# Polysketch attention with a sentence-level expert layer: k and q of the first batch in two loads each, kv turned whole, and output stores of two quarters each

## The chip, the cores and the metric

The kernel runs on one core of a Trainium2 chip. The metric is the device time of one execution in microseconds (us), lower is better. The profile's span of the same execution is 2.0 to 2.1 us shorter than the time.

Each run is marked fast or slow; slow is a run over 1.5% above the fastest of the same kernel. Ratios below are the mean time of one kernel's fast runs over the mean of the fast runs of the kernel before from the same rounds, so they are not quite the ratios of the medians quoted beside them.

## The reference, cut to what matters

```python
def phi(x):                                   # [B, H, S, 32] -> [B, H, S, 64], r = 8
    a = einsum('rd,bhsd->bhsr', S1, x)
    b = einsum('rd,bhsd->bhsr', S2, x)
    return einsum('bhsi,bhsj->bhsij', a, b).reshape(..., r * r)
q_p, k_p = phi(q), phi(k)
kv  = einsum('bhsf,bhsd->bhfd', k_p, v)
z   = k_p.sum(axis=2)
x   = (q_p @ kv) / (q_p @ z + 1e-6)           # per head; then [B, S, H*32]
e   = argmax(x.mean(axis=1) @ w_gate)         # one expert for a whole sentence
out = gate * (relu(x @ w1[e]) @ w2[e])        # [4, 1088, 128] float32
```

There are four batches, four heads and 1088 tokens. The output is 2.23 MB. The experts' weights cannot be loaded before a batch's attention is finished, since the gate picks them.

## The kernel before: the parts that matter

The kernel is a list of operations in a fixed order with a fixed engine for each. It lays a batch's 1088 tokens out as 32 groups (`pp`) of 34 (`x`); the 34 are cut into four quarters of 9, 9, 8 and 8. A chunk of 128 tokens is four quarters by 32 groups, so in the output tile `ob` a quarter lies on 32 partitions.

```python
X0  = (0, 9, 18, 26)                 # where a quarter starts among the 34
LEN = (9, 9, 8, 8)
...
o_s = [plan.add({"ACTQ": 0.4}, lambda: load_s(nc.scalar, 0), bus=0.1),     # S1 from the ACT queue
       plan.add({"POOL": 1.0}, lambda: load_s(nc.gpsimd, 1))]              # S2 from the POOL queue
...
def x_out(eng, i):                                  # attention's result as bf16: tokens in the order (chunk, quarter, group)
    n = LEN[2 * i]
    x = T(xbf)[:].rearrange("p (c a t) -> p a c t", a=4, t=32)[:, 2 * i:2 * i + 2, 0:n]
...
def store(queue, quarters, s=s, ob=ob):             # s: one of three thirds of a batch's chunks
    dst = out[b].rearrange("(pp x) d -> pp (x d)", pp=32)
    for a in quarters:
        m = min(3, LEN[a] - 3 * s)
        lo = X0[a] + 3 * s
        queue.dma_start(dst[:, 128 * lo:128 * (lo + m)], T(ob)[32 * a:32 * a + 32, 0:128 * m])
```

There are 48 stores, four for each third of a batch, each of 32 rows of 1536 bytes (1024 in some). There are four `ob` buffers.

Some words of this document, which counts batches from 0: the *sketch* is the product of k or q with the matrices S1 and S2, which are turned (transposed) on PE first; a *turn* of k or q is a transpose on DVE. The *key products* and *query products* are the outer products `a_i * b_j` of `phi`, made on POOL and DVE. The *numerators* are the products `q_p @ kv` on PE. The engines are PE (TensorE, matrix products), DVE (VectorE), ACT (ScalarE) and POOL (GpSimd). SP, ACT and POOL also issue DMA transfers, each on a queue of its own, and the transfers run on the core's 16 DMA engines.

Of the kernel before, what the change touches and what calls it, by code (L numbers as in the profile page):

```python
# [77 lines left out]
def kernel(  # L78
# [12 lines left out]
    nc = tc.nc  # L91
# [25 lines left out]
        kvr=([P, 64], FP32), kvs=([P, 2, H, 32], FP32), zs=([P, 32], FP32), wq=([P, 96], FP32),  # L117
# [48 lines left out]
    def pre_turned():  # L166
        for i in range(kinds["kT"]):
# [6 lines left out]
    o_pre_turned = plan.add({"DVE": 0.5}, pre_turned)  # L174
    plan.add({"ACT": 1.5}, lambda: nc.scalar.activation(out=tiny[:, 0:4], in_=tiny[:, 4:8], func=AF.Exp),
             after=[o_pre_dve])
    o_s = [plan.add({"ACTQ": 0.4}, lambda: load_s(nc.scalar, 0), bus=0.1),
           plan.add({"POOL": 1.0}, lambda: load_s(nc.gpsimd, 1))]
# [10 lines left out]
    WARM = 5  # L189
    plan.add({"PE": 1.17}, warm_up, after=[o_pre_dve], uses=[wslot], n=2 * WARM)  # L190
# [30 lines left out]
    def attention(b):  # L221
# [4 lines left out]
        def turned(src, ld, tr):  # L226


            def load(lo, hi):
                nc.sync.dma_start(T(ld)[:, 32 * lo:32 * hi],  # L230
                                  src[b].rearrange("h (pp x) d -> (h pp) (x d)", pp=32)[:, 32 * lo:32 * hi])

            whole = b or src is q
            parts = [(0, 34)] if whole else [(0, 18), (18, 34)]
            loads = [add({"SP": 0.4}, lambda lo=lo, hi=hi: load(lo, hi), bus=1.75 if whole else 0.065 * (hi - lo),
                         uses=[ld]) for lo, hi in parts]

            def turn(a, m, n):
                nc.vector.transpose(  # L239
                    out=T(tr)[:, 0:n, a:a + m, :].rearrange("p c a t -> p a c t"),  # L240
                    in_=T(ld)[:, 32 * X0[a]:32 * (X0[a] + m * n)].rearrange("p (a c d) -> p a c d", a=m, d=32))

            turns = [(0, 2, 9, 0), (2, 2, 8, -1)]
            return [add({"DVE": 0.08 + 0.0388 * m * n}, lambda a=a, m=m, n=n: turn(a, m, n),
                        after=[loads[i], o_pre_turned], uses=[ld, tr]) for a, m, n, i in turns]
# [41 lines left out]
        def sketch(ps, tr, w, moving, lo, hi, halves):  # L287

            for c in range(lo, hi):
                for o in halves:  # L290
                    nc.tensor.matmul(cols(ps, w, c)[o:o + 64],  # L291
                                     T(tr)[:, c, o // 32:o // 32 + 2].rearrange("p a t -> p (a t)"), moving)
# [5 lines left out]
        def sketches(ps, tr, w, moving, ts, each, after, uses):  # L298

            if b >= SPLIT:  # L300
                return [plan.add({"PE": 0.1 + 9 * each}, lambda: sketch(ps, tr, w, moving(), 0, 9, (0, 64)),
                                 after=ts + after, uses=[tr] + ps + uses, n=72, form="128x64")]
            first = plan.add({"PE": 0.05 + 4.5 * each}, lambda: sketch(ps, tr, w, moving(), 0, 9, (0,)),
                             after=[ts[0]] + after, uses=[tr] + ps + uses, n=36, form="128x64")
            return [plan.add({"PE": 0.05 + 0.5 * (hi - lo) * each},
                             lambda lo=lo, hi=hi: sketch(ps, tr, w, moving(), lo, hi, (64,)),
                             after=[ts[1], first], uses=[tr, ps[i]] + uses, n=4 * (hi - lo), form="128x64")
                    for i, (lo, hi) in enumerate(thirds)]
# [6 lines left out]
        ks = sketches(kps, kT, 64, lambda: s12[:].rearrange("p t h r -> p (t h r)"), kt, 1.15 / 9, [o_sk], [])  # L315
# [48 lines left out]
        def k_v(s):  # L364
            run.append(s)
            for i, c in enumerate(range(3 * s, 3 * s + 3)):
# [6 lines left out]
               for s in range(3)]  # L373
        kr = add({"DVE": 0.2, "ACT": 0.25}, lambda eng: copy(eng, T(kvr)[:], T(kvps)[:, 0:64]), after=kvm,
                 uses=[kvps, kvr])

        def turn_kv():

            for u in range(2):
                for a in range(4):  # L380
                    nc.tensor.matmul(T(kvt)[32 * a:32 * a + 32, 128 * u:128 * u + 128],
                                     T(kvr)[:, 32 * u:32 * u + 32], ident[:])

        tk = add({"PE": 0.5}, turn_kv, after=[kr], uses=[kvr, kvt], n=32, form="128x32")
# [7 lines left out]
        qs = sketches(qps, qT, 96, lambda: T(wq)[:], qt, 1.38 / 9, [wo, o_sx], [wq])  # L392
# [102 lines left out]
    def experts(b, st):  # L495
# [21 lines left out]
        for k, (i, lo, hi) in enumerate(pieces):  # L517
# [3 lines left out]
            costs = {"POOL": 0.08 + 1.0 * part, "ACT": 0.2 + 0.85 * part, "DVE": 0.12 + 0.62 * part}  # L521
            cw.append(add(costs, lambda eng, i=i, lo=lo, hi=hi: cast(eng, i, lo, hi), after=[lw], uses=[wf, wbf]))
        for s in range(3):
# [56 lines left out]
            def store(queue, quarters, s=s, ob=ob):  # L580
                dst = out[b].rearrange("(pp x) d -> pp (x d)", pp=32)
                for a in quarters:
                    m = min(3, LEN[a] - 3 * s)
                    lo = X0[a] + 3 * s
                    queue.dma_start(dst[:, 128 * lo:128 * (lo + m)], T(ob)[32 * a:32 * a + 32, 0:128 * m])

            if tail:
                add({"SP": 0.9}, lambda store=store: store(nc.sync, (0, 1)), after=oe, uses=[ob], bus=0.4)
                add({"ACTQ": 0.9}, lambda store=store: store(nc.scalar, (2, 3)), after=oe, uses=[ob], bus=0.4)
            else:  # L590
                add({"SP": 1.8}, lambda store=store: store(nc.sync, range(4)), after=oe, uses=[ob], bus=0.8)

    sts = [attention(b) for b in range(B)]
    for b in range(B):
# [3 lines left out]
        6, 14, 5, 3, 15, 0, 39, 4, 8, 2, 1, 32, 7, 16, 9, 10, 17, 18, 11, 72, 12, 21, 13, 19, 24, 20, 22, 27, 23, 41,  # L598
        28, 40, 29, 26, 30, 31, 116, 42, 25, 35, 45, 43, 50, 34, 73, 46, 33, 51, 44, 74, 85, 36, 48, 37, 47, 54, 52,
        75, 38, 57, 118, 60, 92, 49, 55, 117, 77, 53, 58, 119, 160, 76, 63, 67, 56, 81, 79, 59, 121, 82, 120, 83, 61,  # L600
        125, 124, 87, 62, 93, 123, 64, 94, 84, 126, 162, 136, 80, 95, 66, 161, 65, 78, 180, 68, 96, 98, 88, 69, 127,
        163, 99, 122, 97, 204, 70, 128, 100, 86, 71, 138, 165, 206, 164, 101, 89, 168, 129, 137, 169, 90, 103, 139,
        91, 167, 170, 208, 102, 106, 205, 171, 142, 104, 182, 140, 236, 238, 143, 237, 172, 141, 181, 239, 105, 223,
        144, 224, 183, 107, 207, 166, 146, 145, 242, 108, 184, 240, 186, 243, 131, 185, 148, 187, 132, 241, 130, 188,
        225, 133, 173, 212, 209, 147, 226, 134, 213, 245, 135, 244, 149, 190, 189, 227, 151, 246, 228, 109, 150, 192,
        247, 152, 210, 248, 111, 193, 110, 174, 211, 176, 195, 112, 175, 191, 153, 113, 177, 196, 249, 114, 115, 178,
        194, 155, 251, 229, 154, 179, 214, 230, 156, 215, 216, 231, 217, 157, 197, 294, 158, 250, 292, 159, 219, 198,
        257, 199, 233, 258, 279, 285, 252, 218, 280, 286, 281, 232, 282, 268, 234, 259, 269, 283, 260, 220, 235, 284,
        200, 270, 221, 201, 272, 271, 266, 273, 288, 222, 202, 287, 295, 267, 253, 255, 254, 289, 293, 337, 275, 256,
        290, 335, 276, 203, 326, 311, 327, 309, 312, 291, 261, 310, 315, 262, 316, 322, 313, 323, 263, 314, 296, 264,  # L610
        298, 274, 297, 299, 265, 300, 318, 301, 338, 328, 324, 336, 329, 319, 302, 325, 277, 317, 303, 356, 278, 320,
        343, 357, 331, 344, 354, 332, 355, 321, 345, 352, 346, 330, 353, 369, 333, 306, 371, 370, 358, 334, 304, 372,
        359, 305, 341, 307, 339, 342, 361, 308, 362, 340, 360, 367, 363, 365, 368, 349, 348, 364, 366, 347, 373, 350,
        375, 378, 351, 374, 376, 377, 380, 379,
    )
    ENGINES = (
        "2332153200230144220000122333010240001014220000121212222222323222011502124220113330102400010142201222"
        "2222332220210212422011333020240001014220121222233322201102124220113330202400010242201212222333222011"
        "0212414342010202010001401010101000240101010100014424301010202000140201010200024020101010002442410102"
        "010100014010202010002401010101000144242020202010002402010102000240101010100011145"  # L620
    )
    PLACES = (
        0, 1, 11, 0, 0, 0, 0, 0, 0, 0, 0, 1, 10, 0, 0, 1, 0, 0, 11, 0, 10, 0, 1, 0, 0, 0, 0, 0, 1, 12, 0, 0, 1, 2, 0,
        1, 1, 1, 0, 1, 1, 1, 1, 0, 1, 0, 1, 0, 1, 1, 1, 1, 0, 1, 1, 1, 1, 0, 1, 1, 2, 0, 0, 2, 2, 2, 1, 0, 0, 0, 2,
        10, 0, 12, 0, 0, 0, 0, 1, 0, 0, 0, 0, 0, 0, 2, 0, 0, 0, 2, 0, 3, 3, 3, 1, 1, 1, 1, 1, 0, 1, 1, 1, 0, 1, 1, 1,
        1, 1, 1, 1, 1, 1, 0, 1, 1, 1, 2, 1, 0, 0, 2, 1, 2, 2, 0, 0, 2, 1, 1, 1, 1, 1, 1, 1, 0, 1, 0, 2, 1, 0, 0, 1,
        1, 3, 1, 2, 0, 2, 0, 0, 1, 0, 1, 1, 2, 1, 1, 0, 1, 0, 0, 2, 0, 3, 0, 0, 3, 0, 1, 2, 2, 0, 0, 0, 2, 1, 2, 0,
        0, 2, 2, 1, 1, 0, 0, 1, 3, 1, 1, 0, 0, 2, 1, 0, 0, 2, 1, 1, 2, 0, 1, 1, 1, 2, 2, 1, 2, 0, 1, 3,
    )
    WIDE = (156, 200)  # L630
    FILLS = {
        8: (2, 1), 18: (1, 3), 28: (3, 4), 30: (3, 2), 42: (2, 2), 119: (2, 2), 83: (3, 2), 169: (3, 4), 223: (3, 0),
# [38 lines left out]
```

## Time and profile before

| | before |
|---|---|
| time, first three runs | 83.62, 84.59, 87.48 us |
| the profiled execution (a slow one) | 89.07 us, span 87.0 |
| PE busy, share of the span | 74.5 us, 86% |
| output stores | 48, of 48 KB mostly, issued in 0.42 us each |

The prediction shows the main lines of this profile. Two more are of use later. They are the two DMA rows of the page: the span is cut into 40 slices, and for each the first row gives the mean busy share of the core's 16 DMA engines in tenths, the second what they moved in GB/s.

```profile
DMA  1996707038946869931611248693429723424441
GB/s 24 341 265 141 254 0 244 20 82 202 335 166 222 242 222 261 231 91 40 185 39 36 50 107 279 177 347 124 107 71 275 258 74 78 109 64 104 110 111 36
```

Look at the last eight slices, where only output stores are left: 64 to 111 GB/s, at a share of 0.2 to 0.4 (the very last slice is the end of the work, with less). Sixteen engines are far from full there, and PE is busy in most of these slices: the stores go as fast as the work before them delivers.

### The profile page before, as it was taken

To read this page: it belongs to the slowest core of one execution; us is meant where nothing else is said; L and a number is where in the kernel's file an instruction comes from. 1 tells how busy PE (TensorE), PEld (TensorE's weight loads), DVE (VectorE), ACT (ScalarE), POOL (GpSimd) and SP (SyncE) were. 2 spreads that over 40 slices of the span, in tenths; PEclk is the share of its full clock that TensorE was granted. 3 is DMA by queue.
4 is the path that set the end of the run, shared out by engine and by line. 5 is a ranking of instruction groups with operands and counts; after the bars stand their busy time and mean duration, and the time that the engine had idled before them with its cause. 6 is when DMAs were issued, how large, how long until landed. Compare 5 with 4: busy or idle time off the path is not lost.

```text
span 87.0 us, 3463 instructions
## 1 busy us (share of the span) xinstructions
PE 74.5 (86%) x1460; PEld 53.9 (62%) x1460; DVE 58.7 (67%) x131; ACT 42.7 (49%) x94; POOL 36.4 (42%) x37
## 2 busy tenths in 40 slices
PE   3929999999969997999099999999999979999700
PEld 1207837887539856576075747688787856889600
DVE  2403264299995998999999978478964865585200
ACT  3300100233307424948136567679979977945120
POOL 4202595039999999999739700040000000000000
PEclk9999579999999999999999999999999999999999
DMA  1996707038946869931611248693429723424441
GB/s 24 341 265 141 254 0 244 20 82 202 335 166 222 242 222 261 231 91 40 185 39 36 50 107 279 177 347 124 107 71 275 258 74 78 109 64 104 110 111 36
DMA packets 10990, 13.32 MB, mean 153 GB/s; under 512 B 1504, under 2 KB 9184, under 8 KB 10976
## 3 DMA queue, kind: packets, MB, share of 16 engines
q1 hardware_dynamic: 10688, 13.05, 51.4%
q8 instruction: 11, 0.18, 0.9%
q10 hardware_dynamic: 256, 0.07, 0.3%
q14 instruction: 3, 0.02, 0.1%
q0 software_dynamic: 32, 0.00, 0.0%
HBM read 10.89 MB, written 2.23 MB: 151 GB/s over the span
## 4 chain that ended last, share of the span: by engine, by line
PE 48%; DVE 23%; DMA 12%; issue 7%; ACT 4%; SPq 1%; ACTq 0%
DMA wf<-in_moe_w_dram 12%; PE pt L554 12%; PE ps L533 9%; PE ps L447 7%; DVE wbf L217 5%; DVE phT L438 5%; PE ps L291 5%; PE pt L291 4%; PE ps L639 3%; PE pt L187 2%; DVE bc L404 2%; DVE kT L239 2%; DVE den L410 2%; DVE den L409 2%; ACT xbf L460 2%
## 5 line engine op out<-in xcount | busy, mean ns | idle before, releaser
L543 ACT ACTIVATE hT<-ps 128x768 bf16<-128x768 f32 (+1 forms) x33 | 23.9, 762 | 8.3 <-PE ps L533 8.0
L554 PE MATMUL pt<-wbf,hT 128*128 128x128 bf16 (+1 forms) x288 | 20.5, 220 | 2.9 <-DVE wbf L217 2.4
L554 PEld LDWEIGHTS <-hT 128*128 128x128 bf16 (+1 forms) x288 | 17.9, 99 | 6.8 <-issue 4.4
L533 PE MATMUL ps<-xbf,wbf 128*128 128x384 bf16 (+1 forms) x96 | 19.4, 318 | 1.0 <-ACT wbf L215 0.6
L280 POOL TENSOR_TENSOR phk<-kab 128x768 f32<-128x768 f32 x12 | 17.8, 1509 | 2.2 <-DVE kab L217 2.2
L545 DVE TENSOR_SCALAR hT<-ps 128x768 bf16<-128x768 f32 (+1 forms) x15 | 13.9, 946 | 6.2 <-PE ps L533 5.6
L280 POOL TENSOR_TENSOR phq<-qab 128x768 f32<-128x768 f32 x10 | 14.9, 1511 | 6.6 <-DVE qab L413 6.6
L438 DVE STREAM_TRANSPOSE phT<-phq 128x768 f32<-128x768 f32 x12 | 11.1, 948 | 0.0
L533 PEld LDWEIGHTS <-wbf 128*128 128x128 bf16 x96 | 8.1, 99 | 4.7 <-issue 0.8
L460 ACT ACTIVATE xbf<-ps 128x512 bf16<-128x512 f32 (+1 forms) x7 | 4.3, 616 | 5.9 <-PE ps L447 5.9
L447 PE MATMUL ps<-phT,kvs 32*32 32x256 f32 (+1 forms) x256 | 6.5, 399 | 0.7 <-DVE phT L438 0.7
L291 PE MATMUL ps<-wq,qT 128*64 128x96 f32 x120 | 6.8, 250 | 0.3 <-DVE qT L239 0.2
L217 DVE CAST wbf<-wf 128x1024 bf16<-128x1024 f32 x5 | 5.9, 1185 | 1.4 <-DMA wf<-in_moe_w_dram 1.4
L291 PEld LDWEIGHTS ps<-wq,qT 128*64 128x64 f32 x120 | 5.7, 137 | 1.6 <-ACT hT L543 0.5
L239 DVE STREAM_TRANSPOSE kT<-ld 128x576 f32<-128x576 f32 (+1 forms) x8 | 5.8, 729 | 0.2 <-DMA ld<-in_k_dram 0.2
L239 DVE STREAM_TRANSPOSE qT<-ld 128x512 f32<-128x512 f32 (+1 forms) x8 | 5.6, 717 | 0.0
L639 PE MATMUL ps<-warm 128*128 128x512 bf16 x17 | 5.5, 424 | 0.0
L567 ACT ACTIVATE ob<-pt,gate 64x128 f32<-64x128 f32 (+3 forms) x10 | 4.2, 446 | 2.4 <-issue 1.3
L291 PE MATMUL ps<-s,kT 128*64 128x64 f32 x120 | 5.2, 230 | 0.0
L291 PEld LDWEIGHTS ps<-s,kT 128*64 128x64 f32 x120 | 4.5, 142 | 0.8 <-DVE den L409 0.4
L570 DVE TENSOR_SCALAR ob<-pt,gate 128x384 f32<-128x384 f32 (+2 forms) x7 | 3.7, 554 | 1.7 <-DMA out_dram<-ob 1.2
L447 PEld LDWEIGHTS ps<-phT,kvs 32*32 32x32 f32 x256 | 3.4, 103 | 2.3 <-DVE phT L438 0.8
(87 smaller groups left out, 74.2 us busy)
## 6 DMA issues: line engine op xcount, KB each, us to landing
wf<-in_moe_w_dram SPq DMA_DIRECT2D x7, 512.0 KB, 5.8
ld<-in_q_dram SPq DMA_DIRECT2D x4, 544.0 KB, 5.2
out_dram<-ob SPq DMA_DIRECT2D x40, 48.0 KB, 1.6
ld<-in_k_dram SPq DMA_DIRECT2D x3, 544.0 KB, 3.6
vld<-in_v_dram SPq DMA_DIRECT2D x8, 144.0 KB, 4.0
vld<-in_v_dram SPq DMA_DIRECT2D x8, 128.0 KB, 4.1
wf<-in_moe_w_dram SPq DMA_DIRECT2D x2, 256.0 KB, 4.4
ld<-in_k_dram SPq DMA_DIRECT2D x1, 288.0 KB, 2.7
```

Source lines behind the costliest of these rows:

```text
L217: (nc.vector if eng == "DVE" else nc.gpsimd).tensor_copy(o, i)
L239: nc.vector.transpose(out=T(tr)[:, 0:n, a:a + m, :].rearrange("p c a t -> p a c t"), in_=T(ld)[:, 32 * X0[a]:32 * (X0[a] + m * n)].rearran ...
L280: nc.gpsimd.tensor_tensor(out=T(ph)[:, 3 * s:3 * s + 3, :, :].rearrange("p c h (i j) -> p (c h) i j", i=R), in0=view[:, 0].unsqueeze(3).to ...
L291: nc.tensor.matmul(cols(ps, w, c)[o:o + 64], T(tr)[:, c, o // 32:o // 32 + 2].rearrange("p a t -> p (a t)"), moving)
L438: turns = [add({"DVE": 0.97}, lambda s=s: nc.vector.transpose(out=T(phT)[:, :, 3 * s:3 * s + 3, :].rearrange("p f c t -> p c f t"), in_=T( ...
L447: nc.tensor.matmul(T(nps[a // 2])[32 * h:32 * h + 32, a % 2, 0:32 * LEN[a]], T(kvs)[32 * a:32 * a + 32, u, h, :], T(phT)[32 * a:32 * a + 3 ...
L460: nc.scalar.activation(out=x, in_=y, func=AF.Copy, accum_out=T(pool)[:, i:i + 1])
L533: nc.tensor.matmul(T(hp)[:, t, 0:w], T(wbf)[:, 0, 128 * j:128 * j + 128], T(xbf)[:, 384 * s:384 * s + w])
L543: nc.scalar.activation(out=o, in_=i, func=AF.Relu)
L545: nc.vector.tensor_scalar(out=o, in0=i, scalar1=0.0, scalar2=None, op0=MAXOP)
L554: nc.tensor.matmul(T(ops)[0:n, 128 * i:128 * i + 128], T(hT)[:, j, 128 * i:128 * i + n], T(wbf)[:, 1, 128 * j:128 * j + 128], start=(j == ...
L639: nc.tensor.matmul(singles[bank][:, :] if bank < 2 else pairs[bank - 2][:, 0, :], warm[:, 0:128], warm[:, :])
```

## The change

Its intent, as the diff lets one read it: bring the first sketch and the first query products forward, keep the weight casts of the first two batches off DVE, turn kv in two transposes instead of sixteen small products, and halve the number of stores. The diff, cut to its core:

```diff
-    o_s = [plan.add({"ACTQ": 0.4}, lambda: load_s(nc.scalar, 0), bus=0.1),
-           plan.add({"POOL": 1.0}, lambda: load_s(nc.gpsimd, 1))]
+    o_s = [plan.add({"ACTQ": 0.5}, lambda: load_s(nc.scalar, 0), bus=0.1),
+           plan.add({"ACTQ": 0.5}, lambda: load_s(nc.scalar, 1), bus=0.1)]
...
-            whole = b or src is q
+            whole = b > 0
             parts = [(0, 34)] if whole else [(0, 18), (18, 34)]
... (the first batch's sketches go by thirds of the chunks, over both token halves at once)
-                for a in range(4):
-                    nc.tensor.matmul(T(kvt)[32 * a:32 * a + 32, 128 * u:128 * u + 128],
-                                     T(kvr)[:, 32 * u:32 * u + 32], ident[:])
+                nc.tensor.transpose(T(kvt)[:, 128 * u:128 * u + 128], T(kvr)[:, u].rearrange("p a f -> p (a f)"), ident[:])
...
-            costs = {"POOL": 0.08 + 1.0 * part, "ACT": 0.2 + 0.85 * part, "DVE": 0.12 + 0.62 * part}
+            costs = {"POOL": 0.08 + 1.0 * part, "ACT": 0.2 + 0.85 * part}
+            if b > 1:
+                costs["DVE"] = 0.12 + 0.62 * part
...
-                    m = min(3, LEN[a] - 3 * s)
-                    lo = X0[a] + 3 * s
-                    queue.dma_start(dst[:, 128 * lo:128 * (lo + m)], T(ob)[32 * a:32 * a + 32, 0:128 * m])
+                    n, m, x = LEN[a], min(3, LEN[a] - 3 * s), X0[a]
+                    queue.dma_start(
+                        dst[:, 128 * x:128 * (x + 2 * n)].rearrange("pp (a y) -> a pp y", a=2)[
+                            :, :, 384 * s:384 * s + 128 * m],
+                        T(ob)[32 * a:32 * a + 64, 0:128 * m])
...
-                add({"SP": 1.8}, lambda store=store: store(nc.sync, range(4)), after=oe, uses=[ob], bus=0.8)
+                add({"SP": 0.9}, lambda store=store: store(nc.sync, (0, 2)), after=oe, uses=[ob], bus=0.8)
... (and a new order of operations and assignment of engines)
```

The line `"pp (a y) -> a pp y"` lists the destination as 2 quarters by 32 groups by 384 elements, with the 2 outermost.

## The prediction

> **What bounds the kernel now.** I read the busy table first: no engine is full over the whole span, so the kernel has stages. The slices and the group table then say which engine sets which stage, and the timeline shows the joints.
>
> ```profile
> span 87.0 us, 3463 instructions
> PE 74.5 (86%) x1460; PEld 53.9 (62%) x1460; DVE 58.7 (67%) x131; ACT 42.7 (49%) x94; POOL 36.4 (42%) x37
> PE   3929999999969997999099999999999979999700
> POOL 4202595039999999999739700040000000000000
> PEclk9999579999999999999999999999999999999999
> ```
>
> The columns are fortieths of the span, 2.18 us each. Up to about 19 us the start is a chain of waits. From 19 to 49 us POOL is full (22 products of 1.5 us). From 44 us to the end PE is full with the expert products. The joints, from the timeline (start, duration, engine, line, what; the bracket is the idle time before it and what ended that):
>
> ```profile
> 6.37 0.25 PE L193 MATMUL pt<-ident,sraw 16*32 16x16 f32 x8 [1.71 <-issue]
> 18.88 1.51 POOL L280 TENSOR_TENSOR phq<-qab 128x768 f32<-128x768 f32 x1 [4.64 <-DVE qab L413]
> 20.66 1.27 PE L291 MATMUL ps<-s,kT 128*64 128x64 f32 x36
> ...
> 38.56 4.46 POOL L280 TENSOR_TENSOR phq<-qab 128x768 f32<-128x768 f32 x3
> 40.40 3.17 DVE L217 CAST wbf<-wf 128x1024 bf16<-128x1024 f32 x1
> 43.62 1.05 PE L554 MATMUL pt<-wbf,hT 128*128 128x128 bf16 x16 [2.36 <-DVE wbf L217]
> 45.01 1.51 POOL L280 TENSOR_TENSOR phq<-qab 128x768 f32<-128x768 f32 x1 [1.99 <-DVE qab L413]
> ```
>
> See three things. PE cannot turn S before 6.37 us, because S2's load from the POOL queue takes 5.0 us. POOL stands for 4.64 us until the first query product. One DVE cast takes 3.17 us where others take 0.69, and PE (2.36) and POOL (1.99) wait for it.
>
> This profile is of a slow execution (its run took 89.07 us); the three timed runs are 83.62 to 87.48. Reported time less span is 2.07 us. A normal span is therefore about 82.5.
>
> The output is small beside the rest today:
>
> ```profile
> out_dram<-ob SPq DMA_DIRECT2D x40, 48.0 KB, 1.6
> HBM read 10.89 MB, written 2.23 MB: 151 GB/s over the span
> 2.50:3.50 1.00, 1.00 (x4) 0.30 (x2) 0.28 (x1) 0.36 (x2) 0.38 (x2) 1.00 0.99 379
> ```
>
> A store lands in 1.6 us. The last line is a window during the first loads: its two last columns say that 16 DMA engines, 99% busy, moved 379 GB/s. That is 23.7 GB/s for one engine.
>
> **What the Trainium skill says.** (1) "DMA: Bandwidth & Descriptors", section "Why a DMA increments its semaphore by 16 and not by 1": a copy runs on the largest number k of engines, at most 16, that divides the slowest dimension of both sides that isn't of size 1, and on the hardware queues these are the lowest-numbered k; the semaphore gets 16-k at once and then one per engine. The trace agrees where it can be tested: the 8-row load of S1 made one jump at 1.42 us and eight updates from 2.00 to 2.10, so k was 8; ordinary transfers make sixteen. (2) Same page, "Rules for kernel authors": an outermost dimension of size c below 16 confines the whole copy to at most c engines. No transfer of the kernel before has one below 8. (3) "SBUF — State Buffer", "Who interferes with whom": a DVE cast in a two-port mode and a GpSimd instruction exclude each other for a whole instruction. The trace agrees: the slow cast began at 40.40 and ended at 43.57, 0.55 us after POOL's row of three ended at 43.02. (4) "TensorE: Matmul & The Clock Gate", "What's actually happening": half clock until about 3.4 us of sustained work. The trace agrees: PEclk falls to 5 in the fifth slice, after the wait for S.
>
> **The change part by part.**
>
> *Start.* S2 goes to the ACT hardware queue. S1 landed 1.36 us after its issue there, so I expect both by about 3 us, against 6.3. Then key transposes set the start of the sketches: q's first part is loaded ahead of k, so k's second half lands at about 4.5 and its first at 5.3 us. Two transposes of 0.70 and 0.78 follow, and the sketch starts at about 6.4 instead of 6.96. The sketches now alternate the two token halves, as the later batches do: those take 1.27 us for 36 records, where the first took about 3.4 at changing clock. By DVE's order I add: first product at about 7.5 (was 9.79), k copies and one product of 1.08 on DVE, zs 10.2, wq 10.4, first third of q, two other transposes of 0.75, sum, reciprocal and scale 0.64. The first query product comes at about 14 instead of 18.88. Worth about 4 us in the chain.
>
> *Casts.* For the first two batches the cast leaves DVE for ACT (0.62 + 0.62 + 1.05) and POOL after its products. The 3.17 us row goes; PE gets back up to 2.4. POOL's number of products stays 22.
>
> *kv turned whole.* Sixteen records of 0.64 us become two transposes, about 0.25; the copy before them grows from 0.21 to about 0.37. Net 0.2 to 0.3 us per batch, mostly hidden.
>
> *Stores, issue.* 48 stores become 24. At 0.42 us an issue that is up to 10 us of SP's queue, but SP was not what PE waited for (its only visible waits on stores are 1.2 us before a DVE ob row at the tail). Worth 0.5.
>
> Sum without the next point: 4 + 2.4 + 0.5 + about 0.3, less 1 to 2 for overlap with PE's own full stage: span about 80 of this slow execution's 87, or a time of about 80.
>
> *Stores, engines.* The new store's destination has dimensions 2 x 32 x 384 with the 2 outermost; its source has 64 partitions. By (1), k is 2. All output then goes through two of sixteen engines: 2.23 MB / 2 / 23.7 GB/s = 47 us of each, where today it is 6 us of each of 16. This can't be spread over the kernel. In SP's order only four stores come before the last batch's weights; those wait for the last gate. PE work from the second batch's numerators to that gate sums to about 14 us in both orders. I put those numerators at 39 to 40 us (45.49 before, less the start and the cast), so the weights are issued at about 55 and the remaining twenty stores follow. Already moved: 0.16 MB (last third of batch one) and 0.20 MB. Left: 1.87 MB / 2 / 23.7 = 39.4 us. The last weights, 1.05 MB over 16 engines, are 2.8 us of each ahead of them. PE makes a third of a batch, 196 KB, in some 2.6 us; two engines need 4.1, so they stay behind and never run dry. End: 55.5 + 2.8 + 39.4 + 1.3 for landing = 99, and 101 as a time. The four ob buffers fill; ACT, DVE and finally PE wait for stores. All gains at the start only move the start of this queue.
>
> **The rivals.** (A) The stores spread over all 16 engines anyway, for instance because the outer pair is folded away on its way to the queue. Then the gains above count: about 80 us. For it: this is a whole re-tuned schedule whose other parts repair waits that the trace plainly shows. Against it: the built program carries the 2 outermost, and S1's nine semaphore updates show the rule at work. (B) Two engines, but faster alone than sixteen together. Packets of 1536 bytes took 64 to 65 ns at the least, which is again 23.6 GB/s, so I see little room; at 27 GB/s the queue would take 34.5 and the time be about 96. (C) Two engines, and slower: half of the stores' packets took 90 to 120 ns. At 89 ns each, the median, the queue takes about 53 us, and the time is near 114. I take those as first packets of short bursts. (D) A cast or DVE row meets POOL's lock again, or PE loses its clock in stalls. Both hide behind the store queue if that bounds; in (A) they cost 1 to 3 us.
>
> **Range and chances.** I give two engines 0.86. That is slower in every size I can make of it. (A) has 0.14, mostly faster. Point 101; with the queue's start uncertain by 3 us and its rate by 10%, 94 to 111.
>
> **What would show it right or wrong.** The mean DMA share of 16 engines low (about 2 of 16 busy) in the last 35 us, with 45 to 50 GB/s moved; stores landing in 4 us and more, later ones many times that; ob rows on ACT and DVE waiting for stores, and the chain of waits ending in a run of out_dram transfers. The first query product near 14 us, no cast above 1.1 us and S turned by 4 us would show the gains. If stores still land in about 2 us, the whole verdict is wrong, and the time is near 80.

## The result, and the profile after

The changed kernel took 103.83 us in the median (103.44 to 104.44, four runs, all fast), against 86.03 for before (83.62 to 88.8, four runs). The ratio of the fast runs is 1.235, with a 95% interval of 1.219 to 1.251. It is slower by about 18 us in the medians, and by 20 in the fast runs.

The page of the changed kernel, first its clock and DMA rows (40 slices of 2.5 us) and then its chain of waits, the work that ended last, as shares of the span by engine and by line:

```profile
span 101.4 us, 3288 instructions
PE   5928998979999499999999999999853503000000
PEclk9999999999999999999999999999999955555555
DMA  2995749708569804328377581111111111111110
GB/s 77 315 252 167 252 112 309 278 15 250 202 191 241 202 5 126 101 31 309 122 231 233 161 293 48 56 51 49 50 50 57 49 50 50 51 49 50 50 51 21
...
PE 30%; DMA 30%; DVE 9%; POOL 6%; issue 4%; ACT 3%; SPq 2%; ACTq 0%; DVEq 0%; POOLq 0%
DMA out_dram<-ob 20%; DMA ld<-in_k_dram 10%; PE ps L440 6%; PE ps L291 6%; PE ps L528 5%; PE pt L549 5%; POOL phq L280 3%; POOL phk L280 3%; PE pt L362 2%; DVE kT L239 2%; DVE hT L540 2%; ACT hT L538 1%; PE ps L637 1%; DVE ob L565 1%; PE pt L467 1%
```

From the 25th slice, 60 us, to the end the DMA row is a flat 1 and the GB/s row stands at about 50. Compare the rows of before: there the same bytes went at 64 to 111 GB/s. The chain now has the transfer `out_dram<-ob` as its largest entry, 20%; before it did not appear. The waits of the trace (engine, line, what it waited for, us in total, times, longest):

```profile
DVE ob L565 <- DMA out_dram<-ob: 9.9, 5, 3.3
ACT ob L562 <- DMA out_dram<-ob: 8.6, 1, 8.6
PE pt L549 <- DVE ob L565: 6.3, 3, 3.3
```

The rows that scale the output wait for a free `ob` buffer, hence for a store, and PE waits for those rows. Windows of 5 us of the same execution (busy time and instructions per engine, granted clock, DMA share, GB/s):

```profile
80.00:85.00 5.00, 1.55 (x16) 1.16 (x16) 0.96 (x2) 0.00 (x0) 0.00 (x0) 0.63 0.13 50
85.00:90.00 5.00, 0.00 (x0) 0.00 (x0) 0.35 (x1) 0.37 (x1) 0.00 (x0) 0.50 0.13 50
95.00:100.00 5.00, 0.00 (x0) 0.00 (x0) 0.00 (x0) 0.00 (x0) 0.00 (x0) 0.50 0.13 49
```

From 90 us on nothing computes at all. A share of 0.13 is 2 engines of 16 (2/16 = 0.125), and 49.6 GB/s over two is 24.8 GB/s for each. PE's last product ends at 84.82 us, and the span ends 16.6 us later. In the traces of this kernel with stores over sixteen engines (experiments 1, 5 and 10) that distance is 4.1 to 4.4 us.

The number of engines can also be counted. The pages give the number of packets under 512 bytes. No row of a store is that short. First the changed kernel, then the same kernel with single stores (experiment 10):

```profile
DMA packets 10398, 13.32 MB, mean 131 GB/s; under 512 B 784, under 2 KB 8464, under 8 KB 10384
DMA packets 11118, 13.32 MB, mean 167 GB/s; under 512 B 1504, under 2 KB 9184, under 8 KB 11104
```

The 720 packets between 784 and 1504 are 48 x 16 less 24 x 2, that is, one small packet for each store and each engine it runs on, beside 736 others. The same sum fits every other form of the stores that was run: 736 + 24 x 16 = 1120 (experiment 5), 736 + 48 x 4 = 928 (11), 736 + 12 x 2 + 24 x 16 = 1144 (3) and 736 + 12 x 4 + 8 x 16 = 912 (12). So the outermost dimension of 2 means 2 engines, 4 means 4, and 32 means 16.

The start, from the timeline:

```profile
3.87 0.30 PE L193 MATMUL pt<-ident,sraw 16*32 16x16 f32 x8
6.99 0.78 DVE L239 STREAM_TRANSPOSE kT<-ld 128x576 f32<-128x576 f32 x1 [1.90 <-DMA ld<-in_k_dram]
7.82 0.92 PE L291 MATMUL pt<-s,kT 128*64 128x64 f32 x24 [2.04 <-DVE kT L239]
15.20 1.51 POOL L280 TENSOR_TENSOR phq<-qab 128x768 f32<-128x768 f32 x1 [3.34 <-DVE qab L406]
```

S is turned at 3.87, earlier than before (6.37). But k's first part is turned only at 6.99, and the first sketch starts at 7.82, later than before (6.96). The first query product comes at 15.20 (18.88 before).

### The profile page after: what moved, and what is told of

It reads as the page before. It is cut to its first block, busy times and chain, and to the rows that moved or that the text cites. A ratio compares the mean times of both kernels' runs of the same rounds, so it can differ in the third digit from the quotient of the medians.

```text
span 101.4 us, 3288 instructions
## 1 busy us (share of the span) xinstructions
PE 71.3 (70%) x1391; PEld 51.0 (50%) x1395; DVE 57.3 (56%) x139; ACT 41.2 (41%) x84; POOL 38.5 (38%) x38
## 4 chain that ended last, share of the span: by engine, by line
PE 30%; DMA 30%; DVE 9%; POOL 6%; issue 4%; ACT 3%; SPq 2%; ACTq 0%; DVEq 0%; POOLq 0%
DMA out_dram<-ob 20%; DMA ld<-in_k_dram 10%; PE ps L440 6%; PE ps L291 6%; PE ps L528 5%; PE pt L549 5%; POOL phq L280 3%; POOL phk L280 3%; PE pt L362 2%; DVE kT L239 2%; DVE hT L540 2%; ACT hT L538 1%; PE ps L637 1%; DVE ob L565 1%; PE pt L467 1%
## 5 line engine op out<-in xcount | busy, mean ns | idle before, releaser
L280 POOL TENSOR_TENSOR phk<-kab 128x768 f32<-128x768 f32 x11 | 16.4, 1514 | 4.5 <-DVE kab L217 3.7
L280 POOL TENSOR_TENSOR phq<-qab 128x768 f32<-128x768 f32 x11 | 16.4, 1514 | 4.1 <-DVE qab L406 4.1
L540 DVE TENSOR_SCALAR hT<-ps 128x768 bf16<-128x768 f32 (+1 forms) x14 | 12.6, 915 | 2.4 <-PE ps L528 2.2
L565 DVE TENSOR_SCALAR ob<-pt,gate 128x384 f32<-128x384 f32 (+3 forms) x14 | 6.6, 486 | 12.9 <-DMA out_dram<-ob 9.9
L217 POOL CAST wbf<-wf 128x1024 bf16<-128x1024 f32 x4 | 4.1, 1040 | 14.6 <-PE pt L549 12.2
L239 DVE STREAM_TRANSPOSE kT<-ld 128x512 f32<-128x512 f32 (+1 forms) x8 | 5.8, 730 | 2.6 <-DMA ld<-in_k_dram 2.6
L239 DVE STREAM_TRANSPOSE qT<-ld 128x576 f32<-128x576 f32 (+1 forms) x8 | 5.7, 723 | 2.0 <-DMA ld<-in_q_dram 1.9
L362 PE MATMUL pt<-phk,vld 128*32 128x64 f32 x216 | 4.7, 222 | 1.6 <-POOL phq L280 1.5
L562 ACT ACTIVATE ob<-pt,gate 128x384 f32<-128x384 f32 (+1 forms) x3 | 1.5, 515 | 9.7 <-DMA out_dram<-ob 8.6
L362 PEld LDWEIGHTS pt<-phk,vld 128*32 128x32 f32 x216 | 3.5, 109 | 3.0 <-POOL phq L280 1.9
```

Of the source, the lines that this page charges most:

```text
L239: nc.vector.transpose(out=T(tr)[:, 0:n, a:a + m, :].rearrange("p c a t -> p a c t"), in_=T(ld)[:, 32 * X0[a]:32 * (X0[a] + m * n)].rearran ...
L280: nc.gpsimd.tensor_tensor(out=T(ph)[:, 3 * s:3 * s + 3, :, :].rearrange("p c h (i j) -> p (c h) i j", i=R), in0=view[:, 0].unsqueeze(3).to ...
L362: nc.tensor.matmul(T(kvps)[32 * h:32 * h + 32, 0:64], T(vld)[:, h, c, :], T(phk)[:, c, h, :], start=(len(run) == 1 and i == 0), stop=(len( ...
L540: nc.vector.tensor_scalar(out=o, in0=i, scalar1=0.0, scalar2=None, op0=MAXOP)
L565: nc.vector.tensor_scalar_mul(T(ob)[0:n, lo:hi], T(ops)[0:n, lo:hi], g[0:n])
```

## The experiments

Two questions had to be settled. First, is it the two engines, and if so is it the outermost 2 that causes them? Second, what is the rest of the change worth? The prediction had put that at about 6 us.

Experiments 1 to 4 ran with before at 86.12 us (84.76 to 89.18, eight runs).

**1. Single stores in the changed kernel.** Everything of the change stays except the stores.

```diff
-                    queue.dma_start(dst[...].rearrange("pp (a y) -> a pp y", a=2)[...], T(ob)[32 * a:32 * a + 64, 0:128 * m])
+                    queue.dma_start(dst[:, 128 * lo:128 * (lo + m)], T(ob)[32 * a:32 * a + 32, 0:128 * m])
-    ... store(nc.sync, (0, 2)) ...
+    ... store(nc.sync, range(4)) ...
```

> The changed kernel, with the stores of the kernel before (one quarter each, four per group), all else as changed. Theory (two engines): stores land in under 3 us again, the end is set by PE and not by stores, and the time is 78 to 83 us. Rival (the new order of work is itself slower, the stores only a symptom): over 95 us.

Measured: 86.28 us in the median (84.71, 86.09, 86.46, 87.99; only the first of these is fast, so there is no ratio). By the medians the stores alone cost 17.5 us, which is the whole slowdown. But 78 to 83 was a miss: here the rest of the change showed no gain over before. That opened the second question.

**2. The two-quarter stores in the kernel before.** The reverse: only the stores of the change, nothing else.

```diff
-                    queue.dma_start(dst[:, 128 * lo:128 * (lo + m)], T(ob)[32 * a:32 * a + 32, 0:128 * m])
+                    queue.dma_start(dst[...].rearrange("pp (a y) -> a pp y", a=2)[...], T(ob)[32 * a:32 * a + 64, 0:128 * m])
```

> The kernel before, with the two-quarter stores alone. Theory (two engines): from the second group on, about 59 us, 2.06 MB of stores go through two engines at the 24.8 GB/s each that the changed kernel's steady 49 to 50 GB/s shows: 41.6 us, with the last weights 2.7 and 1.3 for landing a span of 103 and a time of 102 to 107 us, DMA share 0.13 in the last 30 us. Rival (the new order is at fault): within 2 us of the kernel before.

Measured: 107.4 us, ratio 1.263 (1.224 to 1.302). Its DMA rows (slices of 2.6 us) end like those of the changed kernel:

```profile
DMA  2999719947799526018783158311111111111110
GB/s 51 325 224 204 236 45 228 284 149 232 221 269 214 134 57 160 17 28 246 212 268 138 37 149 242 114 52 49 51 56 50 51 50 49 51 50 49 50 50 18
```

The store form is enough by itself. The kernel before loses 21 us by it.

**3. One pair and two singles.** In the changed kernel, quarters 0 and 1 go as one store, and 2 and 3 alone.

```diff
-    ... store(nc.sync, (0, 2)) ...
+    ... store(nc.sync, (0,)), single(nc.sync, (2, 3)) ...
```

> The changed kernel with only the first two quarters of each group as one store and the other two as single stores. Theory (time follows the bytes through two engines): after the last weights 0.98 MB of pairs, 19.8 us of each of two engines, plus 2.2 for their share of the singles and 2.8 for weights, from 59 us: a span near 85, a time of 84 to 89 us. Rival (each new store is slow to issue on SP, 0.6 us[...]): 36 issues in place of 24 cost no less in all, so about the time of one quarter each, or slower than the full change; not in between.

Measured: 86.55 us (85.74, 86.01, 87.09, 90.9), ratio 1.018 (0.988 to 1.048). The time is in the range, but it cannot be told from experiment 1's. If half of the output goes through two engines, that is 1.11 MB / 49.6 GB/s = 22.5 us of each. Most of this fits beside the expert products, which take some 28 us. Not all of it does: in its trace (a fast run) the span ends 6.9 us after PE's last product, where it is 4.1 to 4.4 with single stores.

**4. The second store of each third from the ACT queue.**

```diff
-    ... store(nc.sync, (0, 2)) ...
+    ... store(nc.sync, (0,)), store(nc.scalar, (2,)) ...
```

> The changed kernel with the second store of each group issued from ACT instead of SP. Theory (both queues use the same two engines): no gain, 101 to 107 us, 49 to 51 GB/s in the last 30 us. Rival (one queue, or SP's issuing, is what is slow): two queues move nearly twice as much, 85 to 92 us.

Measured: 103.79 us in its single run. A window near its end:

```profile
85.00:90.00 5.00, 1.01 (x8) 0.74 (x7) 0.59 (x2) 0.08 (x1) 0.00 (x0) 0.50 0.13 50
```

A second queue adds no engine: share 0.13 and 50 GB/s again.

Experiments 5, 6, 7 and 9 ran together, beside eleven runs of before (median 85.62, 84.15 to 89.09).

**5. Two-quarter stores with an outermost 32.** The number of stores, their bytes, their row length, their 64 source partitions and their slow issue stay. Only the order of listing changes: the two quarters of a pair now alternate on the partitions. The result is correct.

```diff
-            x = T(xbf)[:].rearrange("p (c a t) -> p a c t", a=4, t=32)[:, 2 * i:2 * i + 2, 0:n]
+            x = T(xbf)[:].rearrange("p (c i t a) -> p i a c t", i=2, t=32, a=2)[:, i, :, 0:n]
...
-                    ... .rearrange("pp (a y) -> a pp y", a=2)[:, :, 384 * s:384 * s + 128 * m],
+                    ... .rearrange("pp (a y) -> pp a y", a=2)[:, :, 384 * s:384 * s + 128 * m],
```

> The changed kernel, whose two-quarter stores are kept (24 issues, the same bytes, the same rows of 1536 bytes, the same slow form of issue), but the tokens of a pair of quarters lie alternately on the 64 partitions, so that the store's outermost dimension is 32 and not 2. Theory (the outermost dimension of 2 puts each store on two engines): the time falls to that of the kernel with single stores or a little under it, 83.5 to 87 us, and the last 15 us move 75 GB/s and more at shares spread over all engines. Rival (it is the pairing itself, the 64-partition source or the slower issue, that costs): it stays above 95 us.

Measured: 84.29 us (83.64 to 88.29, six runs), ratio 0.9915 (0.980 to 1.003) to before. That is 19.5 us less than the changed kernel, from the order of two dimensions. The rows of its page, span 81.6 us:

```profile
DMA  1989875596087466841620894892983422234332
GB/s 16 310 279 190 287 237 159 160 329 221 19 277 209 142 205 186 214 115 27 194 71 8 227 285 109 263 336 51 296 317 85 100 53 66 62 93 105 73 94 61
```

The tail is back to 53 to 105 GB/s. The 75 GB/s that the expectation put were missed in part: in the last 15 us it is 56, 78 and 92 GB/s by thirds, at shares of 0.24 to 0.38. With the count of small packets (1120, so 16 engines for a store) this settles the first question: pairing, the 64-partition source and the slower issue are all still here, and the time is not lost. The issue is indeed slower per store, but that is harmless. The lines of the trace for the stores of before and of this kernel (shortest, median and longest duration in ns of one issue, first and last start):

```profile
L585 SPq DMA_DIRECT2D out_dram<-ob x46: 314/419/1154, 46.5 to 83.9; - x46
```

```profile
L579 SPq DMA_DIRECT2D out_dram<-ob x23: 533/586/1694, 45.4 to 78.2; - x23
```

**6. The kernel before, once more.** The trace that the prediction was read from is of a slow execution. This run is for a second one.

> The kernel before, unchanged, for a second trace of it, because the one read for the prediction is of an execution of 89.1 us where ordinary ones take 84 to 87. If the part of the start's gain that did not reach the end (the first-sketch kernel with single stores ran in 86.3, where 80 was expected) was read off a slow execution, then a trace of 84 to 86 us has the last chunk's last attention product (batch 3's numerators) at 48 to 51 us and not at 53.4. If the gain was real at that point and lost behind it, they are again at 53 and the time behind them is shorter than the 33 us of the slow trace.

Measured: 85.86 us, span 83.8 (a single run, so of unknown state). The timeline, to be laid beside the lines in the prediction:

```profile
4.67 0.25 PE L193 MATMUL pt<-ident,sraw 16*32 16x16 f32 x8 [0.17 <-issue]
5.26 0.91 PE L291 MATMUL pt<-s,kT 128*64 128x64 f32 x12
15.67 2.98 POOL L280 TENSOR_TENSOR phq<-qab 128x768 f32<-128x768 f32 x2 [3.46 <-DVE qab L413]
37.61 1.54 DVE L217 CAST wbf<-wf 128x1024 bf16<-128x1024 f32 x1
39.20 1.05 PE L554 MATMUL pt<-wbf,hT 128*128 128x128 bf16 x16 [0.77 <-DVE wbf L217]
```

S is turned at 4.67 us, where the slow execution had 6.37. The first query product starts at 15.67, where that had 18.88. The cast takes 1.54, where that had 3.17. The load of S2 on the POOL queue landed 5.0 us after its issue in the slow trace. In this one, and in the traces of experiments 2 and 9, which have the same load, it took 3.3, 3.1 and 4.0. Batch 3's numerators begin at 49.84 us; the slow trace has 53.44, the changed kernel 49.15. So the first alternative of the expectation holds. Of the 3.2 us between the two first query products, 1.7 come from S. Another 0.9 come from the sketch, which took 3.6 us in the slow trace (6.96 to 10.59, with the clock row at 5) and 2.7 here (5.26 to 7.97). What is left, 0.6 us, stays open. Most of the predicted gain was a property of the execution that had been profiled.

**7. The k loads ahead of the q loads**, on top of experiment 5. In the changed kernel 288 KB of q stand in the queue ahead of k.

```diff
-        1, 38, 6, 0, 2, 15, 5, 8, 4, 3, 14, 7, 39, 31, 40, 9, 10, 17, 11, 16, 12, 13, ...
+        1, 14, 6, 0, 2, 15, 5, 8, 4, 3, 38, 7, 39, 31, 16, 9, 10, 17, 11, 40, 12, 13, ...   (14, 15: k; 38: q; 16, 40: their turns)
```

> The interleaved kernel with both k loads of batch 0 ahead of both q loads in the queue, and their turns in that order. In the changed kernel 288 KB of q go first, and k's first part lands only at 6.96 us, so the sketch starts at 7.8, later than before the change. Theory (bytes ahead in the queue set the first sketch): k is there by 5.3 to 5.8, the sketch starts at 6.0 to 6.6, and the end moves by 0.5 to 1.5 us (82.5 to 86). Rival (the start has slack that the later stages absorb): the sketch starts earlier, but the time stays within 0.5 us of the interleaved kernel.

Measured: 83.41 us (81.43 to 86.85; only the 81.43 is fast, so no ratio). The time is in the theory's range, 0.9 us under experiment 5's median, but with one fast run the two alternatives cannot be told apart by it. In the trace, which is of the slowest execution (86.85 us), the first third of the sketch starts at 5.83, earlier than expected. The others were held by something else:

```profile
6.70 0.78 DVE L239 STREAM_TRANSPOSE qT<-ld 128x576 f32<-128x576 f32 x1 [1.30 <-DMA ld<-in_q_dram]
7.40 0.25 DVE L217 COPY s1r<-pt 128x128 f32<-128x128 f32 x1
7.71 0.57 PE L291 MATMUL pt<-s,kT 128*64 128x64 f32 x12 [1.31 <-DVE s1r L217]
```

The copy empties the accumulator bank that the second third needs. On DVE it stands behind a turn of q, and that turn now waits for its load.

**8. That copy ahead of the turn of q**, on top of experiment 7 (run beside eleven runs of before with a median of 85.7).

```diff
-        ... 39, 31, 16, 9, 10, 17, 11, 40, 12, 13, 19, ...
+        ... 39, 31, 16, 9, 10, 17, 11, 12, 13, 40, 19, ...     (13: the copy; 40: the turn of q)
```

> The kernel with k ahead of q, and on DVE the turn of q's first half now behind the copy of the turned sketch matrix. With k first the first third of the sketch ran at 5.83 us, but the second waited until 7.71 for that copy, which stood in DVE's order behind a turn that waited for q's load until 6.70. Theory: the three thirds now run one after the other from about 5.8 to 7.2, 1 to 1.5 us earlier than with q first, and the time is 0.3 to 1.5 us below that of the kernel with k first (82 to 83.5). Rival (slack behind it): the sketch is done earlier and the time stays within 0.3 us of 83.4.

Measured: 82.99 us (81.7 to 84.31, six runs), ratio 0.9675 (0.955 to 0.980), correct. The thirds of the sketch now follow each other:

```profile
5.87 1.16 PE L291 MATMUL pt<-s,kT 128*64 128x64 f32 x24
5.98 0.29 DVE L217 COPY s1r<-pt 128x128 f32<-128x128 f32 x1 [0.74 <-PE pt L208]
6.19 0.77 DVE L239 STREAM_TRANSPOSE qT<-ld 128x576 f32<-128x576 f32 x1
6.87 0.52 PE L291 MATMUL ps<-s,kT 128*64 128x64 f32 x12
```

This version is faster than the kernel before and than the changed kernel. How much of it is this last swap stays open: its median is 0.4 us under that of experiment 7, and the two were not run in the same rounds.

**9. Only the cast moved.** In the kernel before, batch 0's second weight cast goes from DVE to ACT.

```diff
     ops = plan.order(ORDER, ENGINES, PLACES, WIDE)
+    casts[2].eng = "ACT"        # casts: the weight casts in the order of the program
```

> The kernel before with one thing moved: the cast of batch 0's second expert weights (128x1024) runs on ACT and not on DVE, as it does in the changed kernel. In the trace of before this cast took 3.17 us on DVE beside other work of GpSimd and held PE for 2.4 us. Theory of the prediction (the stall is part of ordinary executions and on the path): 1 to 2.5 us faster than before, 83.6 to 85.2 us. Rival (the long row belongs to that slow execution, or PE has slack there): within 0.7 us of before.

Measured: 85.07 us (84.28 to 86.24, six runs), ratio 1.001 (0.991 to 1.011). The rival holds: moving this cast is worth nothing that could be seen, within 1%. PE's wait of 2.36 us in the slow trace is 0.77 in that of experiment 6. In the trace of this run it is gone, and batch 3's numerators still begin at 49.88 us, as they did in experiment 6 (49.84): later stages absorb it.

**10. Single stores in the changed kernel, once more**, the same kernel as in experiment 1, in the call of experiment 8.

> The changed kernel with single-quarter stores once more, with more rounds and for a trace of an ordinary execution, as its first trace fell in a slow one. Theory: the gain that was missing (80 expected, 86.3 measured) was never there, because the start of the kernel before was read off a slow execution: batch 0's attention products start at about 20.5 to 21 us and batch 3's at 48.5 to 49.5, against 21.4 and 49.8 in the ordinary trace of before, and the time is 84 to 86 us, 0 to 1.5 under before. Rival (single stores themselves cost something at the end): the products start as early as in the interleaved kernel (20.5, 49.1), but the time is over 1 us above its 84.3.

Measured: 84.03 us (81.66, 82.19, 83.99, 84.06, 84.07, 88.99; two are fast, no ratio). The median is in the theory's range, just; the trace is not. In it (a fast run, span 79.6) batch 0's numerators start at 19.28 and batch 3's at 47.35, over 1 us ahead of the theory's range. k landed early there, with the same order of loads: the first sketch starts at 6.36, where the changed kernel's trace has 7.82. So in this execution a gain of 2.5 us over experiment 6 does reach batch 3's numerators, and "never there" is too strong. What the change is worth without the pairs is not settled: 1.7 us by the medians (85.7 less 84.03), 3.1 by fast runs alone (85.07 of six less 81.93 of two), 0.8 by the fast runs of experiment 5, and nothing by the medians of experiment 1. It also shows that 24 issues instead of 48 bring nothing that could be seen: 84.29 us in experiment 5 and 84.03 here. They were run at other times.

**11. Four engines: an outermost 4 in single stores.** Wrong on purpose (the rows are permuted).

```diff
-    queue.dma_start(dst[:, 128 * lo:128 * (lo + m)], T(ob)...)
+    queue.dma_start(dst[:, 128 * lo:128 * (lo + m)].rearrange("(e f) y -> f e y", f=4), T(ob)...)
```

> A dose of the number of engines: the kernel with single-quarter stores, whose 32 rows are listed with an outermost dimension of 4 (4 x 8 rows of the same 1536 bytes, 48 issues). It puts the rows in another order than the source has them, so the result is wrong on purpose. Theory (the outermost dimension sets the number of engines): at most 4 x 24.8 = 99 GB/s move when only stores are in flight, at a mean share of about 0.25; the stores need 2.23 MB / 99 GB/s = 22.5 us in all, of which most are hidden, so the time is 85 to 90 us. Rival (only an outermost dimension of 2 is bad, or single rows are free to go anywhere): shares of 0.3 and more with over 110 GB/s in the last stretch and a time within 0.5 us of the kernel with plain single stores.

Measured: 89.4 us (87.69 to 92.66, four runs), ratio 1.039 (1.025 to 1.054). The time and the share are as expected, the rate is not. A window of its last stretch, and the line of its stores (the profile is of a slow execution, 92.66 us):

```profile
75.00:80.00 5.00, 5.00 (x72) 4.32 (x70) 2.64 (x5) 2.85 (x4) 0.00 (x0) 1.00 0.23 71
L580 SPq DMA_DIRECT2D out_dram<-ob x46: 602/616/797, 49.4 to 87.0; - x46
```

The share of 0.23 is just under 4 of 16 engines, but 71 GB/s is less than 4 x 24.8 = 99. SP issues a store in 0.616 us here. In the tail its row of 38 stores lasted 25.7 us, of which 38 x 0.616 = 23.4 us were issue. That is 0.68 us for a store of 46 thousand bytes in the mean (49 at most), or 69 to 73 GB/s, so SP's issue looked like the limit. But a share of 0.23 is nine tenths of four engines' time, so the engines were not far from theirs. PE was done at 81.1, and the stores took until 90.6.

**12. Four engines with few issues.** All four quarters go in one store with an outermost 4, and the ninth chunk of two quarters separately, in 20 issues. Wrong on purpose again; all bytes are written.

```diff
+    queue.dma_start(dst[:, 0:4096].rearrange("pp (a y) -> a pp y", a=4)[:, :, 384 * s:384 * s + 128 * m], T(ob)[:, 0:128 * m])
```

> The changed kernel with all four quarters of a group in one store, whose destination has an outermost dimension of 4 (4 x 32 rows of up to 1536 bytes; the last chunk of two quarters goes separately, and the rows land in other places than they should: wrong on purpose; all 2.23 MB are still written). In the dose with 4 x 8 rows the last stretch moved only 72 GB/s, though four engines at the 24.8 of one in the changed kernel would move 99. There SP issued a store every 0.62 us, and 48 KB per 0.65 us is 74 GB/s. Theory (SP's issue was the limit there, the engines were not): with 20 issues instead of 48 the last stretch reaches 90 to 99 GB/s at a share of about 0.25, and the time falls to 84 to 87 us. Rival (four engines give only 18 GB/s each): 70 to 76 GB/s again, and 87 to 91 us.

Measured: 86.69 us (86.01 to 90.03, seven runs), ratio 1.017 (1.011 to 1.023) to before, which stood at 85.33. The time is in the theory's range and under the rival's. The rate is not shown as cleanly: the profile caught a slow execution, and its last windows read

```profile
70.00:75.00 5.00, 5.00 (x67) 4.12 (x65) 3.82 (x7) 3.42 (x5) 0.00 (x0) 1.00 0.25 70
75.00:80.00 5.00, 4.62 (x66) 3.98 (x64) 2.54 (x5) 2.84 (x4) 0.00 (x0) 1.00 0.27 87
80.00:85.00 5.00, 0.61 (x8) 0.43 (x7) 0.36 (x2) 0.37 (x1) 0.00 (x0) 0.93 0.28 80
```

with several slices of 0.4 us at 98 to 102 GB/s between emptier ones. Four engines do reach about 100, but not all the time. Fewer issues took 2.7 us off experiment 11's median (1.9 between the fast runs), so its issue seems to have been part of its cost; how the rest divides is left open. For the question at hand the row of doses is clear. The runs are of different calls, with before at 85.3 to 86.1 in each. The last column is read from the traces and depends less on fast and slow runs:

| engines for the stores | kernel | time, us | ratio to before | from PE's last product to the end of the span, us |
|---|---|---|---|---|
| 2 | changed kernel | 103.8 | 1.235 | 16.6 |
| 2 for half of the stores, 16 for the rest | experiment 3 | 86.6 | 1.018 | 6.9 |
| 4 | experiments 11, 12 | 89.4, 86.7 | 1.039, 1.017 | 9.5, 7.2 |
| 16 | experiments 5, 10 | 84.3, 84.0 | 0.992, none | 4.3, 4.1 |

## Why the prediction was right, and where it was not

*Two engines (right).* This step carried the verdict, and it is shown from four sides. The count of small packets gives 2 engines for a store. The store form alone makes the kernel before slow (experiment 2). The changed kernel without it is not slow (1, 10). And with the same stores in another order of dimensions the loss is gone (5).

*The rate (slightly off).* The estimate of 23.7 GB/s per engine came from sixteen busy engines. Measured were 24.8.

*When the store queue starts and ends (right, off by 2 us, and partly by luck).* Batch 1's numerators were put at 39 to 40 us and came at 39.19. That hit is luck in part: the prediction took 5.5 to 6.5 us off the slow trace's 45.49 for the start and the cast, but in experiment 6 the kernel before has them at 41.07, so 4.4 us of the distance belong to the slow execution and only 1.9 to the change. The last weights were put at 55 and were issued at 55.60 and 56.23. At 60 us about 2.0 MB of output were still to move, where the prediction had 1.87 MB from 58.3. 2.0 MB / 49.6 GB/s = 40.3 us from 60 gives 100.3, and the landing of the last store is still to come; measured was 101.4, predicted 99. Two errors partly cancel: later and more bytes at the predicted rate would have ended 4 us later than predicted, and the higher rate gave 2 of these back. The time of 103.8 lies 2.8 us above the predicted 101.

*What stands still meanwhile (right).* The prediction let the four `ob` buffers fill, and ACT, DVE and PE wait for stores. The three lines of waits show that. Against experiment 5's fast trace the span is 19.8 us longer. PE's end moves by 7.5 us of that (84.82 against 77.33), and the stores behind it take 12.3 us more (16.6 against 4.3).

*"Worth about 4 us in the chain" (wrong).* The step subtracted the changed kernel's start from one slow execution of the kernel before, in which the S2 load took 5.0 us. In the trace of experiment 6 the first query product comes at 15.67, so against it the changed kernel's 15.20 gains 0.5 us, not 4. One pair of traces is little, so here are all. The kernel before, also with the pairs or with the cast moved, has 15.65, 15.67 and 16.32, beside the 18.88 that the prediction read. The start of the changed kernel, whatever the stores, has 13.75, 13.90, 14.65, 14.83, 15.20, 16.52, 16.59 and 16.69. So the 14 that was predicted does occur. What failed is the 18.88 that it was taken from: by the middle values (15.0 against 16.0) the start gains about 1 us, and it scatters by 3. The prediction had said that the profile was of a slow execution, but corrected only the total for it and not the single waits. Two terms inside it were also too hopeful for the changed kernel's trace. k's first part was put at 5.3 us and was turned only at 6.99, because 288 KB of q and then k's other part stand ahead of it in the queue. The first product was put at 7.5 and came at 8.88. The same order of loads let the sketch start at 6.36 in experiment 10, so the queue is not all of it. Experiments 7 and 8 show that with k first the sketch starts at 5.8.

*"The 3.17 us row goes; PE gets back up to 2.4" (wrong in size).* The row did go: no cast in the changed kernel's trace takes over 1.05 us. But in the trace of experiment 6 it took 1.54, and removing it alone is worth nothing that could be seen (experiment 9). In the trace of experiment 6 the cast ended at 39.15, within a row of six POOL products (35.61 to 45.04), so it did not have to wait for the row's end; in the slow trace it ended only after POOL's row.

*The sum for sixteen engines (a slip).* 4 + 2.4 + 0.5 + 0.3 less 1 to 2 is 5.2 to 6.2. That leaves a span of 81 to 82 of the slow execution's 87.0, so a time of 83 to 84, and not 80 for both. The prediction's "22 products" between 19 and 49 us are 19; the other three come before 15 us. Neither changes the verdict.

*kv turned whole (small, as said, and smaller).* The turn fell from 0.64 to 0.44 us, not to 0.25, and the copy ahead of it grew from 0.21 to 0.37. The net is 0.04 us per batch, where 0.2 to 0.3 was put.

*24 stores instead of 48, "worth 0.5" (not seen).* Experiments 5 and 10 differ by 0.3 us, in the other direction and within their scatter.

*The rivals.* (A), sixteen engines after all, is refuted. Its time of 80 was too low as well: with sixteen engines the kernel takes 84 in the median (81.7 at the least), for the reasons above. (B), 27 GB/s per engine, and (C), 89 ns per packet, are refuted by the steady 49 to 50 GB/s. (D), a lost clock, happened: the clock row falls to 5 from 81 us on. But that is behind the store queue: PE's last eight products took 1.01 us in place of 0.61 (experiment 5), 16.6 us before the end. The other half of (D), a cast held up by POOL, did not come back.

## What to carry to other kernels

Write down the dimensions of both sides of a DMA as the built program lists them, and look at the outermost: an outermost 2 or 4 confined the whole transfer to that many engines here, and a steady DMA share of 0.13 (2 of 16) with an output transfer heading the chain of waits is how it looks in a profile. Putting a larger dimension outermost (here by alternating the two quarters on the partitions) keeps the fewer, larger stores, at no cost that could be seen. When the profile is of a slow execution, take a second trace before a gain is subtracted from single waits of it; here 2.6 to 3.2 us of the gain read off the first one were a property of that one execution. Two traces are few, too: in eight traces of one start the first query product scattered by 3 us.

## What the Trainium skill lacked or had wrong

- "DMA: Bandwidth & Descriptors", section "Specifications", of the Trainium skill gives about 27 GiB/s (29 GB/s) for an engine. Two engines that did nothing but these stores from 65 us on, for over 30 us and in rows of up to 1536 bytes, moved 49 to 50 GB/s, so 24.8 GB/s each. The page's rule for the number of engines held exactly (share 0.13 with an outermost 2, and the count of small packets for outermost dimensions of 2, 4 and 32). What it doesn't say is what fewer engines cost: four for the stores made 86.7 to 89.4 us of 84, and only two made 103.8.
- The same page's section "Rules for kernel authors" says that spreading DMAs over several queues doesn't help bandwidth. Experiment 4 agrees (50 GB/s and 103.79 us with two queues). It was not wrong, but there is nothing on what an issue costs by its form: on SP the median was 0.419 us for a store of 32 rows with one row dimension, and with two it was 0.512 (2 x 32, experiment 4), 0.586 (32 x 2, experiment 5) and 0.616 (4 x 8, experiment 11).
- No page used here gives the spread of one and the same small load over several executions. The 1 KB load of S2 from the POOL queue landed 3.1, 3.3, 4.0 and 5.0 us after its issue in four traces. The slowest of them was in the trace that the prediction read, where S was turned 1.7 us later than in that of experiment 6.
